# A windowed attention feeding a rational MLP on one core: every engine's order written by hand, the first loads in the order of need, and a prologue of its own

## The chip, the cores and the metric

The kernel runs on one core of one Trainium2 chip. The metric is the device time of one execution in microseconds (us). The kernel before has a median of 319.73 us over three runs (317.39 to 325.65). A program on one core has no second die to compare with, so "fast" means only that a run lies within 1.5% of the fastest of its kernel. The profiled execution of before has a span of 318.6 us; the measured time of an execution lies about 1 to 2 us above its span.

## The reference

```python
B, H, S, D = 4, 8, 768, 64; n_sink, window = 4, 128
keep = (key < n_sink) | ((query - key >= 0) & (query - key < window))
x = softmax(where(keep, q @ k.T / sqrt(D), -1e9)) @ v      # (B*S, H*D) = (3072, 512)
h = x @ w_in                                               # 512 -> 2048
P = a0 + a1*h + a2*h**2 + a3*h**3
Q = 1 + |b0|*|h| + |b1|*h**2
out = (P / (Q + 1e-6)) @ w_out                             # 2048 -> 512, float32
```

## The kernel before

The work goes in 12 steps of 256 tokens. A step has 4 pairs of heads for the attention; the MLP halves a step into two units of 1024 hidden features, so there are 24 units. PE makes scores, the weighted sum of v and both projections; ACT (ScalarE) makes the exponentials, copies h out of PSUM and forms 1/Q as exp(-ln Q); DVE (VectorE) makes the masks, the normalization and the polynomials. One iteration of the program's loop takes one unit from each of several steps in flight, and a scheduler may move instructions of an engine against the text.

```python
ps_hp = ...tile_pool(name="ps_h", bufs=2, space=PSUM)   # first projection
ps_sp = ...tile_pool(name="ps_s", bufs=1, space=PSUM)   # scores
ps_mp = ...tile_pool(name="ps_m", bufs=2, space=PSUM)   # all else, ps_out too
...
def load_q(tile_i):             # GpSimd's queue, cast fp32 -> bf16 on the way; k and v too
    nc.gpsimd.dma_start(out=t_, in_=q[...])
def turn_q(tile_i):             # queries turned by DMA, issued from SP
    nc.sync.dma_start_transpose(out=qT_fix[b % 2][...], in_=q_bf.pop(tile_i)...)
def turn_x(s, grp):             # attention output turned by DMA, issued from SP
    for n in range(NTS):
        nc.sync.dma_start_transpose(out=xblk[s][...], in_=x_n[s][...])
def square(i):                  # half of the squares on each engine
    if i % 2 == 0: nc.scalar.activation(out=sq[i], in_=hb[i], func=AF.Square)
    else:          nc.vector.tensor_tensor(out=sq[i], in0=hb[i], in1=hb[i], op=ALU.mult)
...
for i in range(-3, NU + 4):     # s_q, s_a: the steps whose scores, whose sums are made
    scores(s_q, 2 * grp_q); log_den(i - 1); even(i - 1); odd(i - 1)
    project_in(i, 0); attend(s_a, 2 * grp_a); odd_h(i - 1)
    scores(s_q, 2 * grp_q + 1); recip_den(i - 1); project_in(i, 1)
    attend(s_a, 2 * grp_a + 1); turn_x(s_a, grp_a)
    load_v(s_q + 1); numerator(i - 1); mask(s_q, grp_q)          # conditions cut
    magnitude(i); square(i); denominator(i); project_out(.., 0)
    turn_q(2 * s_q + 3); turn_q(2 * s_q + 4); turn_k(s_q + 1)    # every second iteration
    gate(i - 1); project_out(.., 1)
```

The softmax here doesn't subtract the row's maximum and nothing guards it: scores larger than these inputs give would overflow.

Of the kernel before, what the change touches and what calls it, by code (L numbers as in the profile page):

```python
# [17 lines left out]
def kernel(  # L18
# [13 lines left out]
    nc = tc.nc  # L32
    nc.scalar.preload_act_table_set("natural_log_exp_and_others")
# [17 lines left out]
    NU = 2 * NSTEP  # L51
    inv_sqrt_d = 1.0 / float(D) ** 0.5
# [12 lines left out]
    ps_mp = ctx.enter_context(tc.tile_pool(name="ps_m", bufs=2, space=bass.MemoryType.PSUM))  # L65
# [4 lines left out]
    for n in range(3):  # L70
        t_ = const_pool.tile([P, NPB, NHF, 2, D + 1], BF16, name=f"v_bd_{n}")
        nc.gpsimd.memset(t_, 0.0)
        for e in range(2):
            nc.gpsimd.memset(t_[e * 64:(e + 1) * 64, :, :, e, D:D + 1], 1.0)
        v_fix.append(t_)

    def load_q(tile_i):
        b, T = divmod(tile_i, S // P)
        t_ = a_kv.tile([P, H, D], BF16, tag="q_bf", name="q_bf", bufs=3)
        nc.gpsimd.dma_start(out=t_, in_=q[b, :, T * P:(T + 1) * P, :].rearrange("h p d -> p h d"))  # L80
        q_bf[tile_i] = t_

    def load_k(s):
        b, g = divmod(s, GPB)
        t_ = a_kv.tile([P, NTS, H * D], BF16, tag="k_bf", name="k_bf")
        for t in range(NTS):
            r0 = g * TS + t * P
            nc.gpsimd.dma_start(out=t_[:, t, :].rearrange("p (h d) -> p h d", h=H),  # L88
                                in_=k[b, :, r0:r0 + P, :].rearrange("h p d -> p h d"))
        k_bf[s] = t_  # L90

    def load_v(s):
        b, g = divmod(s, GPB)
        t_ = v_fix[s % 3]
        for h in range(H):
            i, e = divmod(h, 2)
            nc.gpsimd.dma_start(  # L97
                out=t_[e * 64:(e + 1) * 64, i, :, e, 0:D],
                in_=v[b, h, g * TS:(g + 1) * TS, :].rearrange("(j p) d -> p j d", p=64))
        v_bd[s] = t_  # L100
# [3 lines left out]
    nc.sync.dma_start(out=b_bc, in_=moe_b.partition_broadcast(P))  # L104
    a_bc = const_pool.tile([P, 4], FP32, name="a_bc")
    nc.sync.dma_start(out=a_bc, in_=moe_a.partition_broadcast(P))

    for n in range(3):
        load_q(n)
    load_k(0)  # L110
    load_v(0)

# [13 lines left out]

    edge0 = const_pool.tile([P, 2 * NHF, 2, 64], BF16, name="edge0")
    nc.vector.tensor_copy(out=edge0, in_=edge.unsqueeze(1).to_broadcast([P, 2 * NHF, 2, 64]))
    for e in range(2):
        for n in range(2):  # L130
            nc.vector.memset(edge0[e * 64:e * 64 + NS, n * NHF, 0, :], 1.0)
# [11 lines left out]
    sink_edge = const_pool.tile([P, NS], BF16, name="sink_edge")  # L143
    with nc.allow_low_precision(reason="sum of one 1 and zeros"):
        nc.vector.tensor_reduce(out=sink_edge, in_=tri.rearrange("p h c -> p c h"),
                                axis=mybir.AxisListType.X, op=ALU.add)

    babs = const_pool.tile([P, 2], FP32, name="babs")
    nc.scalar.activation(out=babs, in_=b_bc, func=AF.Abs)
    bpos = const_pool.tile([P, 2], FP32, name="bpos")  # L150
    nc.vector.tensor_scalar(out=bpos, in0=babs, scalar1=1e-9, scalar2=None, op0=ALU.max)
    binv = const_pool.tile([P, 2], FP32, name="binv")
    nc.vector.reciprocal(out=binv, in_=bpos)

    csc = const_pool.tile([P, 1], FP32, name="csc")
    nc.vector.tensor_tensor(out=csc, in0=bpos[:, 1:2], in1=binv[:, 0:1], op=ALU.mult)
    cinv = const_pool.tile([P, 1], FP32, name="cinv")
    nc.vector.tensor_tensor(out=cinv, in0=bpos[:, 0:1], in1=binv[:, 1:2], op=ALU.mult)
    qsc = const_pool.tile([P, 1], FP32, name="qsc")
    nc.vector.tensor_tensor(out=qsc, in0=bpos[:, 0:1], in1=cinv, op=ALU.mult)  # L160
    acoef = const_pool.tile([P, 4], FP32, name="acoef")
    nc.vector.tensor_copy(out=acoef[:, 0:1], in_=a_bc[:, 0:1])
    cpow = const_pool.tile([P, 3], FP32, name="cpow")
    nc.vector.tensor_copy(out=cpow[:, 0:1], in_=cinv)
    nc.vector.tensor_tensor(out=cpow[:, 1:2], in0=cinv, in1=cinv, op=ALU.mult)
    nc.vector.tensor_tensor(out=cpow[:, 2:3], in0=cpow[:, 1:2], in1=cinv, op=ALU.mult)
    nc.vector.tensor_tensor(out=acoef[:, 1:4], in0=a_bc[:, 1:4], in1=cpow, op=ALU.mult)
    one_eps = const_pool.tile([P, 1], FP32, name="one_eps")
    nc.vector.memset(one_eps, 1.000001)
    a0, a1, a2, a3 = (acoef[:, n:n + 1] for n in range(4))  # L170


    e_fix = {}
    for grp in range(2):
        for n in range(2):
            t_ = const_pool.tile([P, 2 * NHF * EW + 64], BF16, name=f"e_{grp}_{n}")
            nc.vector.memset(t_, 0.0)
            e_fix[grp, n] = t_
    kT_fix = []
    for n in range(2):  # L180
        t_ = const_pool.tile([P, NPB * NHF, P], BF16, name=f"kT_{n}")
        nc.vector.memset(t_, 0.0)
        kT_fix.append(t_)
    k_sink = []
    for n in range(2):
        t_ = const_pool.tile([P, NPB, P], BF16, name=f"k_sink_{n}")
        nc.vector.memset(t_, 0.0)
        k_sink.append(t_)
    qT_fix = []
    for n in range(2):  # L190
        t_ = const_pool.tile([P, NPB, S + P], BF16, name=f"qT_{n}")
        nc.vector.memset(t_[:, :, S:S + P], 0.0)
        qT_fix.append(t_)

    w_in_sb = [wpool.tile([P, DF], BF16, name=f"w_in_sb_{c}") for c in range(NDMC)]
    w_out_sb = [wpool.tile([P, DM], BF16, name=f"w_out_sb_{c}") for c in range(NFFC)]
    v_sink = const_pool.tile([P, B, H, D + 1], BF16, name="v_sink")
    nc.vector.memset(v_sink, 0.0)

    def load_w_in(half):  # L200
        f0, f1 = half * DF // 2, (half + 1) * DF // 2
        for c in range(NDMC):
            t_f = a_kv.tile([P, DF // 2], FP32, tag="w_in_f", name="w_in_f", bufs=2)
            nc.sync.dma_start(out=t_f, in_=moe_w_in[c * P:(c + 1) * P, f0:f1])
            nc.vector.tensor_scalar(out=w_in_sb[c][:, f0:f1], in0=t_f, scalar1=csc,
                                    scalar2=None, op0=ALU.mult)

    def load_w_out():
        for c in range(NFFC):
            nc.gpsimd.dma_start(out=w_out_sb[c], in_=moe_w_out[c * P:(c + 1) * P, :])  # L210

    def load_v_sink():
        for h in range(H):
            nc.gpsimd.dma_start(out=v_sink[16 * h:16 * h + NS, :, h, 0:D],
                                in_=v[:, h, 0:NS, :].rearrange("b s d -> s b d"))
        for b in range(B):
            nc.vector.tensor_copy(out=v_sink[:, b, :, D], in_=ind)


    def turn_q(tile_i):  # L220
        b, T = divmod(tile_i, S // P)
        nc.sync.dma_start_transpose(out=qT_fix[b % 2][:, :, T * P:(T + 1) * P],
                                    in_=q_bf.pop(tile_i).rearrange("p h d -> p (h d)"))

    def turn_k(s):
# [13 lines left out]
        if g == 0:  # L239
            for i in range(NPB):  # L240
                nc.vector.tensor_copy(
                    out=k_sink[b % 2][:, i, 32 * i:32 * i + 32].rearrange(
                        "p (e s) -> p e s", e=2)[:, :, 0:NS],
                    in_=kT[:, i * NHF, :].rearrange("p (e s) -> p e s", e=2)[:, :, 0:NS])
# [3 lines left out]
    def sink_scores(s):  # L248
# [3 lines left out]
        for i in range(NPB):  # L252
            nc.tensor.matmul(ps[:, c0:TS], lhsT=k_sink[b % 2][:, i, :],
                             rhs=qT_fix[b % 2][:, i, g * TS + c0:(g + 1) * TS],
                             start=(i == 0), stop=(i == NPB - 1))
        t_ = a_x.tile([P, TS], BF16, tag="e_sink", name="e_sink")
# [6 lines left out]
    def scores(s, i):  # L263
# [4 lines left out]
        for n in range(NHF):  # L268
# [3 lines left out]
                             rhs=qT_fix[b % 2][:, i, c:c + 192], start=True, stop=True)  # L272
        data = e_t[:, 64:].rearrange("p (j c) -> p j c", c=EW)[:, il * NHF:(il + 1) * NHF, 0:192]
# [14 lines left out]
    def attend(s, i):  # L288
# [4 lines left out]
        for n in range(NTS):  # L293
# [10 lines left out]
            for m, (l_, r_) in enumerate(terms):  # L304
                nc.tensor.matmul(ps_o[:, n, :], lhsT=l_, rhs=r_.rearrange("p e c -> p (e c)"),  # L305
                                 start=(m == 0), stop=(m == len(terms) - 1))
        if i == 0:
# [12 lines left out]
    def turn_x(s, grp):  # L320
        if grp == 0:
            xblk[s] = xpool.tile([P, NDMC, TS], BF16, tag="xblk", name="xblk")
        for n in range(NTS):
# [6 lines left out]

    def project_in(i, half):
        m, u = divmod(i, 2)
        if half == 0:
            hb[i] = m_sb.tile([P, UW], BF16, tag="hb", name="hb")
        ps_h = ps_hp.tile([P, UC // 2, TS], FP32, tag="ps_h", name="ps_h")
        for n in range(UC // 2):
            fc = u * UC + half * (UC // 2) + n
            for c in range(NDMC):
                nc.tensor.matmul(ps_h[:, n, :], lhsT=w_in_sb[c][:, fc * P:(fc + 1) * P],  # L339
                                 rhs=xblk[m][:, c, :], start=(c == 0), stop=(c == NDMC - 1))  # L340
        w = UW // 2
        nc.scalar.activation(out=hb[i][:, half * w:(half + 1) * w],  # L342
                             in_=ps_h.rearrange("p n c -> p (n c)"), func=AF.Copy)

    def square(i):
        sq[i] = m_sb.tile([P, UW], BF16, tag="sq", name="sq")
        if i % 2 == 0:
# [167 lines left out]
```

## Time and profile before

| | before |
|---|---|
| median time, span | 319.73, 318.6 us |
| first logarithm, fourth logarithm (units 0 and 3) | 61.12, 104.91 us |
| a unit: 3 to 12, 12 to 20 | 10.45, 9.93 us |
| from the last logarithm to the end | 13.0 us |
| DVE, PE, ACT busy | 250.4, 240.5, 212.8 us |

The logarithm of a unit (written lnq) occurs once per unit, so its starts cut the run into fill, units and tail. Most views of before stand in the prediction. In them PE is TensorE, PEld its weight loads, SPq the DMA issues of SyncE. A slice is a fortieth of the span and its digit the busy share in tenths; PEclk is the granted TensorE clock, also in tenths. Three more lines matter later. First, the group of the score matmuls: 192 of them are busy 27.4 us, and PE was idle only 9.4 us just ahead of them, most of that for turned keys (kT).

```profile
L270 PE MATMUL ps_s<-qT,kT 128*128 128x192 bf16 x192 | 27.4, 272 | 9.4 <-DVE kT L237 7.3 <-ACT e L274 1.8
```

Second, SP's issues in order of time (start, duration, queue, line, what): the two last pairs of query turns.

```profile
126.70 2.51 SPq L222 DMA_TRANSPOSE qT<-q_bf  x2
147.85 2.71 SPq L222 DMA_TRANSPOSE qT<-q_bf  x2
```

After 150.6 us before turns no more queries: the scheduler has drawn these issues far ahead of their place in the loop.

### The profile page before, as it was taken

What the parts mean: (1) busy time and instruction counts of PE and PEld (TensorE: products, weight loads), DVE (VectorE), ACT (ScalarE), POOL (GpSimd) and SP (SyncE); (2) the same over time, 40 slices, a digit from 0 to 9 for tenths busy, and PEclk for the clock granted to TensorE, in tenths of its full rate; (3) what the DMA queues carried; (4) which work ended last, traced back from release to release, by engine and by line L of the source; (5) the groups of instructions that cost most, each with busy time, mean ns of one, the idle gap of its engine ahead of it and who ended that gap; (6) DMA issues with size and microseconds to landing.
All of it is one profiled execution on the core that took longest, in us unless ns stands there. A gap on an engine that the chain in (4) does not pass through costs nothing.

```text
span 318.6 us, 5033 instructions
## 1 busy us (share of the span) xinstructions
PE 240.5 (75%) x1920; PEld 167.4 (53%) x1920; DVE 250.4 (79%) x384; ACT 212.8 (67%) x194; POOL 127.1 (40%) x192
## 2 busy tenths in 40 slices
PE   0025448749348969998879989989899898979964
PEld 0014336638224746666647665577575675746521
DVE  7534520769936897899998999999999899897990
ACT  1013014657823993996878978889799897877951
POOL 9986667996884341534540113356200000000000
PEclk9999556979858998999999999999999999999999
DMA  4999999999999996996960627549510111110011
GB/s 132 111 209 192 204 184 151 99 131 103 111 107 136 102 123 84 86 82 86 107 76 17 76 54 56 72 58 107 72 44 22 36 51 49 35 33 33 35 66 66
DMA packets 110775, 28.67 MB, mean 90 GB/s; under 512 B 104608, under 2 KB 106656, under 8 KB 110752
## 3 DMA queue, kind: packets, MB, share of 16 engines
q0 software_dynamic: 78976, 11.56, 58.1%
q1 hardware_dynamic: 31776, 16.79, 23.6%
q8 instruction: 15, 0.25, 0.3%
q14 instruction: 8, 0.07, 0.1%
HBM read 27.30 MB, written 6.29 MB: 105 GB/s over the span
## 4 chain that ended last, share of the span: by engine, by line
DVE 33%; ACT 21%; DMA 19%; PE 10%; issue 7%; POOL 5%; SPq 3%; DVEq 0%; ACTq 0%; POOLq 0%
DMA xblk<-x_n 12%; ACT lnq L379 7%; ACT den L383 6%; DVE den L358 5%; DVE g L388 5%; PE ps_h L339 5%; DVE num L373 4%; DVE sq L370 4%; PE ps_out L398 3%; ACT e L274 3%; SPq L324 3%; DVE den L354 3%; ACT hb L342 3%; DVE num L362 2%; DMA q_bf<-in_q_dram 2%
## 5 line engine op out<-in xcount | busy, mean ns | idle before, releaser
L339 PE MATMUL ps_h<-xblk,w_in_sb 128*128 128x256 bf16 x768 | 98.0, 278 | 30.7 <-DMA xblk<-x_n 30.6
L339 PEld LDWEIGHTS <-w_in_sb 128*128 128x128 bf16 x768 | 74.4, 100 | 45.6 <-DMA xblk<-x_n 28.1
L398 PE MATMUL ps_out<-w_out_sb,g 128*128 128x512 bf16 x384 | 93.5, 391 | 3.7 <-DVE g L388 3.4
L97 POOL DMA_DIRECT2D v_bd<-in_v_dram x96 | 61.8, 663 | 55.4 <-PE ps_o L305 47.3
L274 ACT ACTIVATE e<-ps_s 128x768 bf16<-128x768 f32 x48 | 38.7, 806 | 53.2 <-PE ps_s L270 53.2
L342 ACT ACTIVATE hb<-ps_h 128x1024 bf16<-128x1024 f32 x48 | 48.7, 1018 | 21.1 <-PE ps_h L339 21.1
L398 PEld LDWEIGHTS <-g 128*128 128x128 bf16 x384 | 37.3, 101 | 44.0 <-issue 5.1
L379 ACT ACTIVATE lnq<-den,one_eps,qsc 128x2048 f32<-128x2048 bf16 x24 | 50.2, 2092 | 5.5 <-DVE den L358 5.5
L383 ACT ACTIVATE den<-lnq 128x2048 bf16<-128x2048 f32 x24 | 45.8, 1908 | 0.0
L270 PE MATMUL ps_s<-qT,kT 128*128 128x192 bf16 x192 | 27.4, 272 | 9.4 <-DVE kT L237 7.3
L305 PE MATMUL ps_o<-v_bd,e 128*128 128x130 bf16 x352 | 31.4, 226 | 3.0 <-DMA v_bd<-in_v_dram 1.8
L388 DVE TENSOR_TENSOR g<-num,den 128x2048 bf16<-128x2048 bf16 x24 | 29.4, 1223 | 5.4 <-ACT den L383 5.3
L358 DVE TENSOR_TENSOR den<-den,sq 128x2048 bf16<-128x2048 bf16 x24 | 29.4, 1223 | 2.5 <-ACT sq L348 2.0
L281 DVE TENSOR_TENSOR e<-e,edge 128x1024 bf16<-128x1024 bf16 x24 | 16.2, 675 | 17.7 <-ACT e L274 17.7
L373 DVE TENSOR_TENSOR num<-num,sq 128x2048 bf16<-128x2048 bf16 x24 | 29.3, 1222 | 0.4
L370 DVE TENSOR_TENSOR sq<-sq,hb 128x2048 bf16<-128x2048 bf16 x24 | 29.1, 1214 | 0.1
L305 PEld LDWEIGHTS <-e 128*128 128x128 bf16 x352 | 26.1, 101 | 5.2 <-issue 3.5
L88 POOL DMA_DIRECT2D k_bf<-in_k_dram x24 | 22.2, 931 | 15.9 <-PE ps_kT L232 14.9
L80 POOL DMA_DIRECT2D q_bf<-in_q_dram x24 | 21.7, 906 | 17.2 <-DMA qT<-q_bf 17.2
L270 PEld LDWEIGHTS <-kT 128*128 128x128 bf16 x192 | 18.0, 108 | 16.4 <-DVE kT L237 9.8
L348 ACT ACTIVATE sq<-hb 128x2048 bf16<-128x2048 bf16 x12 | 22.9, 1911 | 0.3
L232 PE MATMUL ps_kT<-ident,k_bf 128*128 128x128 bf16 x96 | 8.1, 233 | 19.9 <-POOL ident masks.py:199 18.9
(56 smaller groups left out, 224.1 us busy)
## 6 DMA issues: line engine op xcount, KB each, us to landing
out_dram<-o_t SPq DMA_DIRECT2D x24, 256.0 KB, 2.1
w_in_f<-in_moe_w_in_dram SPq DMA_DIRECT2D x8, 512.0 KB, 5.8
q_bf<-in_q_dram POOLq DMA_DIRECT2D x24, 128.0 KB, 4.8
k_bf<-in_k_dram POOLq DMA_DIRECT2D x24, 128.0 KB, 4.8
v_bd<-in_v_dram POOLq DMA_DIRECT2D x96, 32.0 KB, 3.8
w_out_sb<-in_moe_w_out_dram POOLq DMA_DIRECT2D x16, 128.0 KB, 6.7
xblk<-x_n SPq DMA_TRANSPOSE x48, 2.5
qT<-q_bf SPq DMA_TRANSPOSE x24, 4.0
```

Of the source, the lines that this page charges most:

```text
L97: nc.gpsimd.dma_start(out=t_[e * 64:(e + 1) * 64, i, :, e, 0:D], in_=v[b, h, g * TS:(g + 1) * TS, :].rearrange("(j p) d -> p j d", p=64))
L270: nc.tensor.matmul(ps[:, n // 2, (n % 2) * 192:(n % 2) * 192 + 192], lhsT=kT_fix[s % 2][:, i * NHF + n, :], rhs=qT_fix[b % 2][:, i, c:c + ...
L274: nc.scalar.activation(out=data.rearrange("p (a n) c -> p a n c", a=2), in_=ps[:, :, 0:384].rearrange("p a (n c) -> p a n c", n=2), func=A ...
L305: nc.tensor.matmul(ps_o[:, n, :], lhsT=l_, rhs=r_.rearrange("p e c -> p (e c)"), start=(m == 0), stop=(m == len(terms) - 1))
L339: nc.tensor.matmul(ps_h[:, n, :], lhsT=w_in_sb[c][:, fc * P:(fc + 1) * P], rhs=xblk[m][:, c, :], start=(c == 0), stop=(c == NDMC - 1))
L342: nc.scalar.activation(out=hb[i][:, half * w:(half + 1) * w], in_=ps_h.rearrange("p n c -> p (n c)"), func=AF.Copy)
L358: nc.vector.tensor_tensor(out=den[i], in0=den[i], in1=sq[i], op=ALU.add)
L373: nc.vector.tensor_tensor(out=num[i], in0=num[i], in1=sq[i], op=ALU.add)
L379: nc.scalar.activation(out=lnq[i], in_=den[i], func=AF.Ln, scale=qsc, bias=one_eps)
L383: nc.scalar.activation(out=den[i], in_=lnq[i], func=AF.Exp, scale=-1.0)
L388: nc.vector.tensor_tensor(out=g_of[m, u], in0=num[i], in1=den[i], op=ALU.mult)
L398: nc.tensor.matmul(ps_out[m, tt], lhsT=g_of[m, u][:, co:co + P], rhs=w_out_sb[fc], start=(fc == 0), stop=(fc == NFFC - 1))
```

## The change

Its intent: give each engine a fixed order, bring the first data in the order in which it is needed, write steps 0 to 2 by hand, and let each part of the elementwise chain start one unit after its projection, so that no engine waits for work of the same iteration.

```diff
+    ctx.enter_context(tc.manual_schedule())
-    ps_mp = ...(name="ps_m", bufs=2, space=PSUM)
+    ps_mp = ...(name="ps_m", bufs=1, space=PSUM)
+    ps_op = ...(name="ps_o", bufs=1, space=PSUM)        # ps_out alone
 def load_q / load_k / load_v:
-        nc.gpsimd.dma_start(...)                        # cast on the way
+        nc.sync.dma_start(fp32 tile) for steps 0..2, cast later on ACT (q) or DVE (k, v)
 def scale_w_in(half):
-            nc.vector.tensor_scalar(out=w_in_sb[c]..., in0=t_f, scalar1=csc, ...)
+            nc.gpsimd.tensor_scalar(out=w_in_sb[c]..., in0=w_f[half, c], scalar1=csc, ...)
 def turn_q: q tiles 0..6 on PE (transpose, copy by DVE); turn_x: steps 0 and 1 on PE
 def square(i):
-        if i % 2 == 0:                                  # ACT, else DVE
+        if i % 4 != 3:
... (constants moved, GpSimd's and DVE's start reordered)
+def iteration(i):
+    store(..)                                           # ACT copy of ps_out, one iteration late
+    scores(s_q, 2 * grp_q); exps(..)
+    chain_1(i - 1)                                      # magnitude, square if i%4==3, denominator
+    project_in(i, 0); log_den(i - 1); copy_in(i, 0)
+    attend(s_a, 2 * grp_a); gate(i - 2); normalize(..)
+    project_in(i, 1); scores(s_q, 2 * grp_q + 1); exps(..)
+    even(i - 1); odd(i - 1); recip_den(i - 1)
+    attend(s_a, 2 * grp_a + 1); normalize(..); turn_x(s_a, grp_a)
+    copy_in(i, 1); project_out(.., 0); odd_h(i - 1); mask(s_q, grp_q)
+    if grp_q == 0: sink_scores(s_q); sink_exps(s_q); load_v(s_q + 1); feed(s_q + 2)
+    if grp_q == 1: turn_qs(s_q + 1); turn_k(s_q + 1)
+    numerator(i - 1); square(i); project_out(.., 1)
+# prologue: casts, turns, scores, attends of steps 0..2 written out (110 lines)
```

## The prediction

> **What bounds the kernel now.** I read the slices first, then the same thing in windows, then the queues, the waits, and the row of one ScalarE instruction in order of time.
>
> ```profile
> PE   0025448749348969998879989989899898979964
> DVE  7534520769936897899998999999999899897990
> PEclk9999556979858998999999999999999999999999
> DMA  4999999999999996996960627549510111110011
> ```
>
> One slice is 8 us. Up to slice 13 (104 us) PE is broken up and its clock is often 5 to 8 tenths; the DMA engines are full. After slice 15 PE and DVE are both at 8 to 9. So there are two kernels: a fill bound by waits for data, and a balanced steady part. Two windows of the steady part (length, then busy time and count of each engine; PEclk, DMA share, GB/s last):
>
> ```profile
> 120.00:200.00 80.00, 73.12 (x618) 51.41 (x616) 73.31 (x107) 64.71 (x60) 26.80 (x39) 0.99 0.72 75
> 200.00:290.00 90.00, 82.56 (x700) 58.71 (x698) 85.83 (x124) 75.94 (x70) 13.92 (x21) 1.00 0.32 51
> ```
>
> DVE is 95% busy in the second, ACT 84%. The work comes in 24 units (half a step each) with one logarithm (lnq) per unit; its starts are the kernel's pulse:
>
> ```profile
> 61.12 2.09 ACT L379 ACTIVATE lnq<-den,one_eps,qsc 128x2048 f32<-128x2048 bf16 x1
> ...
> 104.91 2.09 ACT L379 ACTIVATE lnq<-den,one_eps,qsc 128x2048 f32<-128x2048 bf16 x1
> ...
> 198.92 2.08 ACT L379 ACTIVATE lnq<-den,one_eps,qsc 128x2048 f32<-128x2048 bf16 x1
> ...
> 278.34 2.10 ACT L379 ACTIVATE lnq<-den,one_eps,qsc 128x2048 f32<-128x2048 bf16 x1 [0.81 <-DVE den L358]
> ...
> 305.56 2.10 ACT L379 ACTIVATE lnq<-den,one_eps,qsc 128x2048 f32<-128x2048 bf16 x1 [0.99 <-DVE den L358]
> ```
>
> These are units 0, 3, 12, 20 and 23. The span of 318.6 is 61.1 of fill, 3 units at 14.6, 9 at 10.4, 8 at 9.93, 3 at 9.07 (attention has ended), and 13.0 of tail. Had all ran at 9.93 after unit 0, 18 us would be saved; the fill holds more.
>
> The waits of the fill (total, times, longest) and the queues (packets, MB, share of 16 engines over the span):
>
> ```profile
> PE ps_h L339 <- DMA xblk<-x_n: 30.6, 14, 8.9
> PE ps_kT L232 <- POOL ident masks.py:199: 18.9, 1, 18.9
> PEld L232 <- DMA k_bf<-in_k_dram: 15.6, 1, 15.6
> ```
> ```profile
> q0 software_dynamic: 78976, 11.56, 58.1%
> q1 hardware_dynamic: 31776, 16.79, 23.6%
> ```
>
> The first transpose waits 15.6 us for keys and then to 18.9 us for an identity that GpSimd makes after 13 load issues and six memsets of v_bd. The projection waits 30.6 us for turned x, 21.4 of it before 120 us: with both queues full the x transpose took up to 7.4 us to land, against a median of 2.5. All q, k and v loads go through q0: 58.1% of 318.6 us x 16 / 78976 is 37.5 ns a packet, so one step of 6144 packets costs that queue 14.4 us, and it is busy until about 165 us.
>
> **What the Trainium skill says.** "DMA: Bandwidth & Descriptors", SWDGE vs HWDGE vs iDMA: only the software path (GpSimd) casts in flight, and the two paths feed different internal queues of one engine, served in turn. The trace agrees: the casting loads are all in q0, and where q0 and q1 both run (60 to 75 us) the DMA share is 1.93. So fp32 loads on the hardware queue add a lane but need a cast afterwards. "TensorE: Matmul & The Clock Gate", Part 4: a PE transpose ends in PSUM and needs a copy by DVE; here ps_kT does (684 ns a copy of 1024 columns). Same page, Part 1: PE idling brings the half clock back; the clock above dips so. "GPSIMD Engine Reference", 4.1: one-input work is roughly line-rate there, so I take 1 to 2 us for a 128x1024 scale, an estimate; no row of before has one.
>
> **The change part by part.** It takes the order of every engine from the text (before, a scheduler chose it; the instruction lists of the two differ in nearly every line, though in number hardly: PE 3930 rows against 3842, DVE 355 in both). It loads q, k and v of steps 0 to 2 as fp32 through the hardware queue in the order of need and casts them on ACT and DVE; turns q tiles 0 to 6 and x of steps 0 and 1 on PE instead of by DMA; moves the w_in scaling to GpSimd, half of DVE's squares to ACT, and ps_out to a bank of its own (so the other small PSUM tiles share one bank in place of two); and starts the polynomial of a unit one iteration after its projection. I work out three stretches. "Hops" are the 0.1 to 0.2 us from one engine's end to the next one's start, as between kT's copy at 22.07 and the scores at 22.13, taken generously.
>
> *Fill.* (a) The first issue of keys moves from 9.9 to about 1.3 us, of queries from 6.8 to about 2.2. The same five transfers took 10.4 us in before (6.82 to 17.2); 1.3 + 10.4, plus 2 for v sharing the engines, gives 14. (b) Cast on ACT 0.6, four transposes 0.5, copy about 0.4 (half of ps_kT's 0.684 and a fixed part), hops 0.5: 16. The identity is first on GpSimd now, so that wait is gone. (c) Four score rounds on the single ps_s: the exps of step 0 start 1.7 us apart in before, so 6.9: 23. (d) Four attends through a now single ps_m bank: about 1.0 cold matmuls, 0.18 + 0.42 on DVE, 0.3 hops, 1.9 each, 7.6; two PE turns of x at 1.2: 33. That replaces transposes by DMA that ended at 44.3 and 49.6. (e) Projection 32 matmuls at 0.17 cold (38 took 6.34): 5.5; copy 1.0, square 1.9, den 1.2, hops: 43. w_in needs 2 MB at about 200 GB/s after the queries, near 24, and four scales, near 30: hidden. I allow 3 us for the second step's keys: first lnq at 46 against 61.1. **Saving 15.**
>
> *Units 0 to 3.* Between lnq 0 and 1 DVE does 4 normalizations 2.4, two copies 0.9, two masks 1.4, the polynomial 4.1, casts and kT 3.2, queries 0.9, den 1.9: 14.8. Then 10.5 and 10 with loads still dense: 35 against 43.8. **Saving 9.**
>
> *Steady part.* Removed from DVE: half of its 12 squares, 0.25 x 1.22 = 0.30 a unit; 9.06 units in 90 us gave 85.83 / 9.06 = 9.47, now 9.2. Added to ACT: 0.25 x 1.91 = 0.48 on 8.38, now 8.9. PE by spacing, since its ends are modelled:
>
> ```profile
> 293.37 3.66 PE L339 MATMUL ps_h<-xblk,w_in_sb 128*128 128x256 bf16 x32
> 296.86 7.07 PE L398 MATMUL ps_out<-w_out_sb,g 128*128 128x512 bf16 x32
> ```
>
> Taking off the last one's length, 0.109 and 0.216 us apart: 32 and 16 per unit give 3.5 + 3.45; 18 ps_o at 0.068 are 1.2, 8 ps_s 0.64, kT and sink 0.4: 9.2. Three engines at 9.2, 9.2, 8.9, each waiting for the others in a fixed order: I choose 5% over the largest, 9.65. Nine units at 9.65 instead of 10.45 and eight instead of 9.93: **saving 7 and 2.** Three late units at 8.7: **1.** The tail (ln 2.1, exp 1.9, gate 1.2, 16 matmuls 3.6, copy 0.6, store) keeps its chain: 13.
>
> Sum: 46 + 35 + 86.9 + 77.2 + 26.1 + 13 = 284; the time lies 1.1 above the span (319.73 and 318.6): **285 us**.
>
> Beside the path: DVE loses 6.0 of w_in scaling and gains about 11.5 of casts and copies, all in the fill where it idled.
>
> **Rivals.** *A load-bound fill.* The hardware queue now carries 19456 packets of q, k, v and the w_in in order, with six shared stage buffers: a late cast blocks all behind it, and w_out waits for the keys of step 2. At 37.5 ns a packet steps 0 to 2 take 45 us and w_in about 10, so step 2 lands near 57 and step 3, behind w_out, near 80. For it: DMA is at 9 today. Against: two queues overlap. It would cost 8 to 12 us: 295. *Head-of-line stalls in the fixed order.* One ps_m bank and one ps_out bank make PE wait for DVE and ACT inside each unit; then units stay at 9.93 or reach 10.3: 290 to 297. Against: scores, projections and attends alternate so that a copy has other matmuls beside it. *ACT as the bound.* Three units in four carry a square: 8.38 - 0.96 + 1.91 is 9.3 there, under 9.65. *All better:* 9.3 a unit and lnq 0 at 42: 274.
>
> **Range and chances.** The fill may miss by 8, the unit by 0.35 x 17 = 6; not both the same way as a rule: 273 to 300. Slower than 313 needs the fill gain lost and a worse unit: faster 0.93, same 0.04, slower 0.03.
>
> **What would show it.** lnq 0 near 46 and lnq 3 near 81; then 9.65 apart; the PE waits for xblk down from 30.6 to under 10; PEclk full from about 45 us; ACT about 229 busy. I am wrong if lnq 0 comes after 55 with PE waiting for k, q or v loads, or if units stay above 10 with PE waiting for ps_m or ps_out.

## The result and the profile after

The changed kernel takes 350.19 us in the median of four runs (347.17 to 356.97, the last of them slow), against 319.52 for before in the same rounds. A ratio here is the mean time of one kernel's fast runs over that of the other's fast runs of the same rounds, so it is not quite the ratio of the medians; it is 1.095 (95% interval 1.086 to 1.104). The change is slower by 9.5%. The profiled span is 345.5 us.

The slices (8.6 us each here), then one steady window, in the same columns as the prediction shows for before:

```profile
PE   0446575274886797958874997796869979979675
PEclk9999859558699699969998799999998999999989
```

```profile
200.00:290.00 90.00, 76.03 (x648) 54.83 (x646) 76.78 (x109) 74.55 (x68) 22.41 (x31) 0.98 0.48 65
```

PE starts earlier than in before, but then no engine is full: in 90 us of the steady part DVE works 76.78 us against 85.83 before. Something between the engines makes all of them wait. The logarithms say where:

```profile
50.43 2.09 ACT L457 ACTIVATE lnq<-den,one_eps,qsc 128x2048 f32<-128x2048 bf16 x1 [2.51 <-DVE den L436]
...
102.94 2.10 ACT L457 ACTIVATE lnq<-den,one_eps,qsc 128x2048 f32<-128x2048 bf16 x1 [2.56 <-DVE den L436]
...
214.16 2.08 ACT L457 ACTIVATE lnq<-den,one_eps,qsc 128x2048 f32<-128x2048 bf16 x1
...
303.27 2.09 ACT L457 ACTIVATE lnq<-den,one_eps,qsc 128x2048 f32<-128x2048 bf16 x1 [0.81 <-DVE den L436]
```

These are units 0, 3, 12 and 20. Set against before:

| stretch | before | predicted | after | after less predicted |
|---|---|---|---|---|
| to lnq 0 | 61.1 | 46 | 50.4 | +4.4 |
| units 0 to 3 | 43.8 | 35 | 52.5 | +17.5 |
| units 3 to 12 | 94.0 | 86.9 | 111.2 | +24.3 |
| units 12 to 20 | 79.4 | 77.2 | 89.1 | +11.9 |
| units 20 to 23 | 27.2 | 26.1 | 26.8 | +0.7 |
| tail | 13.0 | 13 | 15.4 | +2.4 |

So 10.7 us were won by the first logarithm, and all but 2.0 of them lost again by the fourth; a unit then takes 12.36 and 11.14 us instead of 10.45 and 9.93. The group of the score matmuls names the place:

```profile
L319 PE MATMUL ps_s<-qT,kT 128*128 128x192 bf16 x192 | 28.7, 276 | 36.7 <-DMA qT<-q_bf 15.0 <-ACT o_t L482 6.9 <-ACT e L331 6.3
```

PE idles 36.7 us ahead of scores instead of 9.4: 27.3 us more, nearly the whole loss of 30. The releaser named first is the turned queries (qT), for 15.0 us. The rest is put down to other engines, and the list alone doesn't show that it has the same cause; the first experiment does. The list of waits has two lines that were not among the long ones of before:

```profile
DVE rec L374 <- PE ps_o L362: 42.0, 34, 5.3
PE ps_s L319 <- DMA qT<-q_bf: 15.0, 8, 4.5
```

DVE now waits 42.0 us for attention sums (8.4 before): work that stands behind the late scores in the fixed order. The chain of waits (start, duration, what) shows how one step's hold-up comes about:

```profile
229.84 0.43 DVE x_n L376
...
230.32 1.17 SPq L397
...
231.54 1.24 SPq L397
...
232.87 1.22 SPq L266
...
234.18 2.41 DMA qT<-q_bf
...
236.64 0.33 PE ps_s L319 x2
```

DVE finishes a normalized x. SP issues two DMA turns of x (L397), 1.2 us each, and only then the turns of the next step's queries (L266), which had been ready (in this run SP never waits for loaded queries there). The first scores of the next iteration stand at the head of PE's order and need those queries. PE therefore waits for a chain that begins with its own last attend. In before the last pair of query turns was issued from 147.85 us on; here the last turn starts at 278.95:

```profile
255.83 2.53 SPq L266 DMA_TRANSPOSE qT<-q_bf  x2
278.95 1.22 SPq L266 DMA_TRANSPOSE qT<-q_bf  x1
```

### The profile page after: what moved, and what is told of

Same layout as the page of the kernel before. It is cut to its first block, busy times and chain, and to the rows that moved or that the text cites. A ratio compares the mean times of both kernels' runs of the same rounds, so it can differ in the third digit from the quotient of the medians.

```text
span 345.5 us, 5116 instructions
## 1 busy us (share of the span) xinstructions
PE 254.3 (74%) x1964; PEld 178.7 (52%) x1964; DVE 254.7 (74%) x372; ACT 229.1 (66%) x207; POOL 127.6 (37%) x165
## 3 DMA queue, kind: packets, MB, share of 16 engines
HBM read 27.30 MB, written 6.29 MB: 97 GB/s over the span
## 4 chain that ended last, share of the span: by engine, by line
PE 38%; DVE 19%; ACT 18%; DMA 13%; SPq 5%; issue 4%; ACTq 0%; DVEq 0%
PE ps_h L412 21%; PE ps_o L362 7%; DMA xblk<-x_n 5%; DMA qT<-q_bf 5%; ACT lnq L457 4%; ACT den L461 4%; PE ps_s L319 4%; PE ps_out L477 4%; ACT hb L420 4%; SPq L397 4%; DVE den L436 3%; ACT sq L426 3%; DVE sq L448 3%; DVE x_n L376 2%; ACT e L331 2%
## 5 line engine op out<-in xcount | busy, mean ns | idle before, releaser
L412 PE MATMUL ps_h<-xblk,w_in_sb 128*128 128x256 bf16 x768 | 106.3, 297 | 11.6 <-DMA xblk<-x_n 11.5
L412 PEld LDWEIGHTS <-w_in_sb 128*128 128x128 bf16 x768 | 79.8, 106 | 28.8 <-DMA xblk<-x_n 14.0
L477 PE MATMUL ps_out<-w_out_sb,g 128*128 128x512 bf16 x384 | 91.0, 384 | 4.9 <-ACT o_t L482 4.9
L127 POOL DMA_DIRECT2D v_bd<-in_v_dram x72 | 47.3, 673 | 101.8 <-PE ps_o L362 99.3
L477 PEld LDWEIGHTS <-g 128*128 128x128 bf16 x384 | 36.7, 99 | 43.0 <-issue 7.7
L319 PE MATMUL ps_s<-qT,kT 128*128 128x192 bf16 x192 | 28.7, 276 | 36.7 <-DMA qT<-q_bf 15.0
L374 DVE RECIPROCAL rec<-ps_o 128x4 f32<-128x4 f32 x48 | 8.7, 181 | 42.0 <-PE ps_o L362 42.0
L362 PE MATMUL ps_o<-v_bd,e 128*128 128x130 bf16 x352 | 32.8, 233 | 5.8 <-DVE x_n L376 4.0
L426 ACT ACTIVATE sq<-hb 128x2048 bf16<-128x2048 bf16 x18 | 34.4, 1913 | 0.4
L245 POOL TENSOR_SCALAR w_in_sb<-w_in_f,csc 128x1024 bf16<-128x1024 f32 x8 | 24.3, 3046 | 2.1 <-DMA w_in_f<-in_moe_w_in_dram 1.9
L376 DVE TENSOR_TENSOR x_n<-ps_o,rec 128x256 bf16<-128x256 f32 x48 | 20.4, 425 | 1.7
```

Of the source, the lines that this page charges most:

```text
L127: nc.gpsimd.dma_start(out=t_[lo:hi, i, :, e, 0:D], in_=src)
L319: nc.tensor.matmul(ps[:, n // 2, (n % 2) * 192:(n % 2) * 192 + 192], lhsT=kT_fix[s % 2][:, i * NHF + n, :], rhs=qT_fix[b % 2][:, i, c:c + ...
L362: nc.tensor.matmul(ps_o[:, n, :], lhsT=l_, rhs=r_.rearrange("p e c -> p (e c)"), start=(m == 0), stop=(m == len(terms) - 1))
L412: nc.tensor.matmul(ps[:, n, :], lhsT=w_in_sb[c][:, fc * P:(fc + 1) * P], rhs=xblk[m][:, c, :], start=(c == 0), stop=(c == NDMC - 1))
L477: nc.tensor.matmul(ps_out[m, tt], lhsT=g_of[m, u][:, co:co + P], rhs=w_out_sb[fc], start=(fc == 0), stop=(fc == NFFC - 1))
```

## The experiments

All fourteen kernels gave correct results. The median of a kernel is over all its runs; those of the change, after_sched and g_fill2_banks hold one slow run each, those of before up to three. Not all groups ran on the same chip, so a difference between two groups is only as good as before's agreement in them (319.5 to 320.8). Before was measured beside each group of runs on the same chip: 320.75, 319.9, 319.92, 320.32 and 320.08 us in the five groups. Times are medians. One kernel that I wanted could not be run: before with the scheduler turned off and nothing else changed. Its text order deadlocks when simulated, so what the bare order of before would cost is open.

| kernel | built on | us | ratio to before |
|---|---|---|---|
| q_early | change | 330.65 | 1.037 (1.028 to 1.045) |
| x_early | change | 356.97 | 1.113 (1.101 to 1.124) |
| q_x_early | change | 355.76 | 1.116 |
| after_sched | change | 337.24 | 1.053 (1.044 to 1.062) |
| q_gate | q_early | 314.34 | 0.985 (0.979 to 0.990) |
| q_pe_x | q_early | 329.88 | 1.033 (1.026 to 1.039) |
| q_banks | q_early | 325.49 | 1.020 (1.013 to 1.026) |
| q_fill | q_early | 331.27 | 1.037 |
| g_fill2 | q_gate | 303.92 | 0.954 (0.946 to 0.963) |
| g_sq | q_gate | 317.28 | 0.996 (0.988 to 1.003) |
| g_banks | q_gate | 305.13 | 0.958 (0.949 to 0.966) |
| g_fill2_banks | g_fill2 | 301.09 | 0.943 (0.936 to 0.950) |
| g_gate_first | g_fill2_banks | 309.28 | 0.970 (0.963 to 0.978) |
| g_sq_split | g_fill2_banks | 297.84 | 0.931 (0.923 to 0.940) |

**q_early: the query turns go ahead of the x turns.**

```diff
 def iteration(i):
+    if has_q and grp_q == 1 and s_q + 1 < NSTEP:
+        turn_qs(s_q + 1)
     ...
     if has_q and grp_q == 1 and s_q + 1 < NSTEP:
-        turn_qs(s_q + 1)
         turn_k(s_q + 1)
```

> The changed kernel with the two DMA turns of q issued at the start of the iteration instead of behind the turn of x; nothing else moved. Theory 1 (the slowdown is the q turn standing last in the SP order: x_n, two x turns of 2.46 us, then a q turn of 1.2 and 2.4 to land, and PE cannot pass the scores that wait for it): a step of 23.0 us loses some 3 us, nine steps, so about 322 us (318 to 328), PE's idle before the scores from 36.7 to about 10. Theory 2 (one bank each for the small PSUM tiles and for ps_out, in a fixed order): no more than 5 us gained, 345 or more. Theory 3 (loads that crowd the DMA engines): the wait moves to x or to loads, 340 or more.

330.65 us: 19.5 less than the change, by moving two issues (18.1 between the means of the fast runs). The time misses the 318 to 328 expected, but the wait goes where it was expected to go. PE's idle time ahead of the scores falls from 36.7 us to

```profile
L319 PE MATMUL ps_s<-qT,kT 128*128 128x192 bf16 x192 | 27.1, 270 | 9.6 <-ACT e L331 6.3 <-DVE kT L281 3.3
```

so the waits that the profile had put down to other engines went with the query turns. That their place behind the x turns is a main cause is thus shown. The wait for turned x rises from 11.5 to 21.2 us, as the third theory had it. What is left is uneven: many units take 9.9 us, but some 12 to 15. At each of those PE waits for turned x:

```profile
208.29 3.09 PE L412 MATMUL ps_h<-xblk,w_in_sb 128*128 128x256 bf16 x14 [4.47 <-DMA xblk<-x_n]
```

The turn it waited for took 6.29 us to land, while a window from 205 to 209 us has a mean DMA share of 2.29, the highest of the neighbourhood. GpSimd had issued v, keys and queries of later steps from 199.3 to 204.7 us, released by the same attends that release the turn of x.

**x_early: attends, normalization and turn of x ahead of the second half of the projection.**

```diff
+    attend(s_a, 2 * grp_a)              # ahead of project_in(i, 0)
     project_in(i, 0) ...
+    attend(s_a, 2 * grp_a + 1)          # ahead of project_in(i, 1)
+    even(i - 1)
+    normalize(s_a, 2 * grp_a + 1); turn_x(s_a, grp_a)
     project_in(i, 1) ...
```

> The changed kernel with both attends of an iteration, their normalizations and the turn of x placed before the second half of the projection and its scores; the turn of q still behind that of x. Theory 1 extended (the loop is x_n, then DMA turns, then the next iteration's first PE work, for x in one iteration and for q in the other): both chains begin about 2 us earlier in every iteration, so about 2 us times some 18 iterations at most, 315 to 330 us. Theory 2 (shared PSUM banks): the two attends now follow each other on one bank with the gate between, so it gets slower, 352 or more.

356.97 us, slower than the change (by 6.6 us between the means of the fast runs; the intervals of the two ratios overlap a little). The two attends now follow each other, and both use the one ps_m bank:

```profile
PE ps_o L362 <- DVE x_n L376: 35.2, 19, 3.6
```

In the change this wait was 4.0 us. The stall at the small bank that the prediction had as a rival is thus real, but only in an order without other matmuls between two attends. The change's own order avoids it.

**q_x_early: both together.** The edit is the sum of the two.

> Both moves together. Theory 1: what is left is the balanced work, some 9.6 us a unit, with the slow fill (lnq 3 at 103 us) and the tail of the changed kernel: 103 + 17 x 9.65 + 3 x 8.9 + 15 is 309 (302 to 318). Theory 2: no faster than the better of the two alone.

355.76 us, the same as x_early: the bank wait (41.6 us in this run) seems to hide what the early queries gain. PE's idle time ahead of the scores does fall, from 18.4 us in x_early to 8.8.

**after_sched: the change without the line that switches the scheduler off.**

```diff
-    ctx.enter_context(tc.manual_schedule())
```

> The changed kernel with the one line taken out that keeps the order as written, so that the scheduler orders every engine as it did for the kernel before; loads, casts, PE turns, banks and the split of squares stay as changed. If the order is at fault: about 310 (300 to 322), below before, since the early loads then pay. If the single PSUM banks or the loads are at fault: 335 or more.

337.24 us, where about 310 was expected if the order alone was at fault. The steady part comes back to nearly that of before: 10.17 us a unit from 12 to 20 (9.93 before, 11.14 in the change). But the fill is worse than that of either kernel: lnq 0 at 64.25 and lnq 3 at 118.25. The written order is therefore not the only thing that costs; the other parts of the change, under the old scheduler, cost 13 us by the fourth unit. One of them is visible there: PE waits 14.7 us in this run for w_in scaled on GpSimd. In the change the same row is

```profile
L245 POOL TENSOR_SCALAR w_in_sb<-w_in_f,csc 128x1024 bf16<-128x1024 f32 x8 | 24.3, 3046 | 2.1 <-DMA w_in_f<-in_moe_w_in_dram 1.9 <-POOL v_bd L188 0.2
```

3.05 us each, against 765 ns on DVE before.

**q_gate: the loads wait until x is turned.** GpSimd copies two elements of the turned x to a spare tile before it issues the loads, so the loads start behind the turn instead of beside it.

```diff
             if s_q + 1 < NSTEP:
+                hold = a_x.tile([P, 2], BF16, tag="hold", name="hold")
+                nc.gpsimd.tensor_copy(out=hold, in_=xblk[s_a][:, 3, P - 1:P + 1])
                 load_v(s_q + 1)
```

> As q_early (330.65 us there), plus one GpSimd copy that reads the turned x of a step before GpSimd issues the next v, k and q loads, so that those loads no longer start together with the x turn that PE waits for. Theory A (in q_early PE waits 21.2 us for x in 10 places because the loads are released by the same attends and crowd the turn): the waits fall to about 5 us and the time to 316 to 322. Theory B (the turn is late in itself: SP issue 2.46 and 2.4 to land): the waits stay near 20 us, 328 or more; if held loads come too late, PE waits for k or v instead and it gets slower.

314.34 us, 16.3 less than q_early and less than before. Between 100 and 300 us the wait for turned x falls from 19.7 us (nine waits, longest 4.5) to

```profile
PE ps_h L412 <- DMA xblk<-x_n: 7.4, 9, 1.3
```

and a unit from 3 to 20 from 10.89 to 10.03 us. The number of waits is the same; each is shorter. That the collision of loads and turns was the second cause is thereby shown. I had not thought of it before the experiments.

**q_pe_x: x of all steps turned on PE, no DMA turn of x.**

```diff
-    NS_PE = 2
+    NS_PE = 12
```

> As q_early, with x of all steps turned on PE through the small PSUM bank and a DVE copy, none by DMA. Theory A and B both take the 21.2 us of x waits away, and what is added is 20 copies of 0.425 us on DVE (8.5 us) and 80 transposes on PE: 314 to 322. Theory 2 (the single small bank binds): the added use of that bank costs as much as it saves, 328 or more.

329.88 us, no gain over q_early, on which it is built. The wait for the DMA is gone and another has its place:

```profile
PE ps_xT L392 <- DVE x_n L376: 26.5, 24, 1.5
```

PE must turn x right behind DVE's normalization and has nothing else at the head of its order: 24 waits of about 1.1 us. The time is the one that the theory of the single small bank expected (328 or more). But x_n is the data of the turn and its writing also frees the bank, so this wait doesn't tell the two apart.

**q_banks: two rotating banks shared by the small tiles and ps_out, as before.**

```diff
-    ps_mp = ...(name="ps_m", bufs=1, ...); ps_op = ...(name="ps_o", bufs=1, ...)
+    ps_mp = ...(name="ps_m", bufs=2, ...)
```

> As q_early, with the two small banks put back as one rotating pair shared by attends, turns, sink scores and ps_out, as in the kernel before. If the single bank for attends and turns binds (theory 2), 322 or less; if not, within 3 us of 330.65, or slower because ps_out now holds one of the pair through two calls.

325.49 us, 5.2 less than q_early, between the two expectations. The gain is in the fill (lnq 0 at 46.56 for 49.93, lnq 3 at 92.26 for 99.33) and in the tail (13.9 us for 17.0). The uneven units remain and take half of it back: 11.19 us a unit from 3 to 20, for 10.89.

**q_fill: the polynomial of unit 0 moved behind the keys, scores and masks of step 2 in the prologue.**

```diff
     copy_in(1, 1)
-    even(0); odd(0); odd_h(0); numerator(0)
     square(1)
     ...
     cast_v(2)
+    even(0); odd(0); odd_h(0); numerator(0)
```

> As q_early, with the polynomial of unit 0 (4 DVE instructions, 4.1 us) moved behind the cast and turn of the third step's keys, its queries, scores and mask. Theory (the fill is a serial chain: PE idles from 59 to 64 us because the cast of k stands behind the polynomial on DVE, and lnq 1 comes 27 us after lnq 0): lnq 1 comes 3 to 4 us earlier and the time is 326 to 328. Rival (PE or loads bind there): no change.

331.27 us, no gain: lnq 1 comes at 78.43 instead of 76.94. Moving one block back leaves the chain as long as it was.

**g_fill2: the prologue of q_gate rewritten.** The casts and turns of the next step stand between the attends of this one, and the turns use the bank of ps_out, which is free in the fill.

```diff
+    attend(0, 0); normalize(0, 0); cast_k(1); turn_k(1, spare=True)
+    attend(0, 1); normalize(0, 1); cast_q(3); turn_q(3, spare=True); turn_x(0, 0)
+    attend(0, 2); normalize(0, 2); cast_q(4); turn_q(4, spare=True)
+    attend(0, 3); normalize(0, 3); turn_x(0, 1)
... (scores of step 1, then the polynomial of unit 0 in pieces between
     the attends of step 1, with the casts and turns of step 2)
```

> On top of q_gate (314.34 us, span 311.7): only the hand-written prologue is rewritten. Casts and turns of the next step's keys and queries stand between the attends of the step before, the turns of the prologue use the bank of ps_out as a second one, the polynomial of unit 0 is cut into pieces between the attends. Theory (the fill is a serial chain through one bank and one order, not a load wait): the stretch from the first logarithm to the second falls from 26.2 us to about 15 to 18, the first stays near 50, and the time to about 303 (297 to 307). Rival (the fill is bound by loads and by the scaling of w_in on GpSimd, which ends near 44 us): the first two logarithms move by less than 3 us and the time stays at 312 to 316.

303.92 us, 10.4 less. The time is as expected, the parts only roughly: from lnq 0 to lnq 1 it is still 19.5 us (15 to 18 expected), and lnq 0, expected to stay near 50, is earlier too. lnq 0 comes at 46.22, lnq 1 at 65.68 (77.25 in q_gate), lnq 3 at 87.88 (99.01). The wait in the change's fill was a chain, one link of which reads like this in PE's rows (last column: idle time and its releaser):

```profile
64.20 1.03 PE L276 MATMUL ps_kT<-ident,k_bf 128*128 128x128 bf16 x8 [5.21 <-DVE k_bf L113]
66.81 0.58 PE L263 MATMUL ps_qT<-ident,q_bf 128*128 128x128 bf16 x4 [1.57 <-DVE kT L281]
67.91 0.59 PE L263 MATMUL ps_qT<-ident,q_bf 128*128 128x128 bf16 x4 [0.52 <-DVE qT L264]
```

Each turn waits for DVE to empty the single ps_m bank, and the first for a cast that stands late on DVE. From 60 to 120 us PE worked at a granted clock of 0.74 in the change; in g_fill2 it is 0.94. It was not a wait for keys: the three casts of keys waited 0.9 us in all for their loads.

**g_sq: the squares shared half and half again, on q_gate.**

```diff
-        if i % 4 != 3:        # ACT
+        if i % 2 == 0:
```

> On top of q_gate: the squares shared half and half by ACT and DVE as in the kernel before (3 of 4 on ACT in the change). If DVE is the bound of the steady units, as the prediction took it, this gives back 0.25 x 1.22 = 0.3 us a unit: +5 to +7 us, about 320. If units are set by chains between engines and not by DVE's work, within 2 us of q_gate, 312 to 317. If ACT were the bound: 305 to 310.

317.28 us, 2.9 more: just outside what I had called "no change", and short of the 5 to 7 us that DVE as the bound would cost. A unit from 2 to 20 is 10.15 us against 10.11 in q_gate; most of the rest lies in fill and tail. Moving a quarter of the squares from ACT to DVE hardly moves the unit, so neither engine's work, summed over all units, sets it. What sets a single unit is taken up in the last run.

**g_banks: two rotating banks, on q_gate.**

> On top of q_gate: the small PSUM tiles and ps_out share two rotating banks, as in the kernel before. On top of q_early this was worth 5 us, all in the fill. Theory (one bank costs only in the fill and the tail): about 309 (306 to 312), with the first logarithm near 46.5, and units 2 to 20 at the 10.1 us of q_gate. Rival (the banks also cost in the steady part and were hidden there by late x turns): units fall to 9.8 or less and the time to 303 to 305.

305.13 us, 9.2 less, more than expected: lnq 0 at 46.72, lnq 3 at 92.81 (99.01), tail 13.8 for 15.3. Units 2 to 20 take 10.13 us, as expected: in the steady part the bank is worth nothing.

**g_fill2_banks: both mends of the fill.** The edit is the sum of the two.

> g_fill2 (303.92 us, span 302.7) with two rotating banks for the small PSUM tiles and ps_out. If the order of the prologue and the bank removed the same wait of the fill, the first logarithms stay at 46, 66 and 76 and the gain is the tail alone: in g_fill2 the last unit waits 3.6 us for the one ps_out bank and then runs at a low clock, 17.8 us from the last logarithm's start to the end against 13.8 in g_banks, so -4: about 300 (298 to 302). If they are two different waits: the third logarithm before 72 and about 294 to 296. If the tail's low clock in g_fill2 was chance: 303.

301.09 us in the median of six runs (five fast, from 299.95 to 304.26), 2.8 less than g_fill2. The tail is 13.9 us against 17.8. In g_fill2 the last unit ran into the one ps_out bank:

```profile
289.44 9.66 PE L477 MATMUL ps_out<-w_out_sb,g 128*128 128x512 bf16 x32 [3.63 <-ACT o_t L482]
```

The gains of the two mends overlap: alone they are 10.4 and 9.2, together 13.3. The profiled run is 3 us above the median of its kernel and has lnq 1 at 69.52, so I do not read its fill closely. The two kernels that follow have the same prologue and banks, with lnq 1 at 66.54 and 65.47 and lnq 2 at 77.06 and 75.64. That is the first alternative: order and bank removed largely the same wait.

**g_gate_first: DVE's product g (1.22 us) moved ahead of the next denominator.**

```diff
+    gate(i - 2)
     chain_1(i - 1)
     ...
     attend(s_a, 2 * grp_a)
-    gate(i - 2)
```

> g_fill2_banks with one line moved: DVE's multiplication g (1.22 us a unit) stands ahead of the magnitude and the denominator of the next unit instead of behind them, so that it runs while DVE waits for ACT's square (1.15 us of idle in every second unit of g_fill2). Same work on all engines. Ring theory (square on ACT, denominator on DVE, logarithm on ACT, in a fixed order): units fall from 10.1 to about 9.5 to 9.8, and the time by 5 to 10 us against g_fill2_banks. Rival (DVE's or ACT's work with the fixed costs of an instruction is already full at 10.1): units stay within 0.1 of 10.1 and the time within 2 us. Third way: the denominator now comes later on DVE in the units where DVE is late, and units rise to 10.4 or more.

309.28 us, 8.2 more: the third way. A unit from 2 to 20 takes 10.45 us. DVE's idle time before the denominator only shrinks from 1.15 to 0.96 us, and where DVE is late anyway the logarithm now waits longer. The theory that g would fit into a gap fell. The trace of g_fill2_banks suggested a new one: units alternate. In the interval that ends with lnq 14 DVE has no idle time (10.12 us; the key turn's copies are in it). In the one that ends with lnq 13 ACT has none (9.78 us), and DVE idles 1.15 us for ACT's square.

**g_sq_split: the square of every odd unit cut in two, half on ACT, half on DVE.**

```diff
 def square(i):
-    if i % 4 != 3: ACT, whole; else DVE, whole
+    w = UW if i % 2 == 0 else UW // 2
+    nc.scalar.activation(out=sq[i][:, 0:w], in_=hb[i][:, 0:w], func=AF.Square)
 def chain_1(i):
     magnitude(i)
-    if i % 4 == 3: square(i)
+    if i % 2 == 1: sq[i][:, w:UW] = hb[i][:, w:UW] ** 2 on DVE
     denominator(i)
```

> g_fill2_banks with the square of every odd unit cut in two, half on ACT and half on DVE, where ACT did it whole in units 1, 5, 9 ... and DVE whole in units 3, 7, 11 ...; the total of each engine's work stays (a little more, for the fixed part of two instructions instead of one). If alternating full engines set the unit (DVE full in the units with a key turn, 10.1; ACT or DVE full in the others, 9.8), the intervals into the odd units fall from 9.8 to about 9.35 and the others stay: about 4 us less than g_fill2_banks, 296 to 298. If a fixed chain of hand-overs or the sum of DVE's work sets it: no change, within 1.5 us of g_fill2_banks (300 to 302.5), or a little more.

297.84 us, within the 296 to 298 expected, 3.3 less than g_fill2_banks and 6.9% less than before. The logarithms of units 12 to 14, in g_fill2_banks and then in g_sq_split:

```profile
181.50 2.10 ACT L456 ACTIVATE lnq<-den,one_eps,qsc 128x2048 f32<-128x2048 bf16 x1 [0.43 <-DVE den L435]
191.28 2.10 ACT L456 ACTIVATE lnq<-den,one_eps,qsc 128x2048 f32<-128x2048 bf16 x1
201.40 2.10 ACT L456 ACTIVATE lnq<-den,one_eps,qsc 128x2048 f32<-128x2048 bf16 x1 [0.57 <-DVE den L435]
```

```profile
176.67 2.10 ACT L459 ACTIVATE lnq<-den,one_eps,qsc 128x2048 f32<-128x2048 bf16 x1 [0.55 <-DVE den L438]
186.01 2.10 ACT L459 ACTIVATE lnq<-den,one_eps,qsc 128x2048 f32<-128x2048 bf16 x1 [0.51 <-DVE den L438]
196.23 2.10 ACT L459 ACTIVATE lnq<-den,one_eps,qsc 128x2048 f32<-128x2048 bf16 x1 [0.68 <-DVE den L438]
```

The interval into the odd unit falls from 9.78 to 9.34 us, where 9.35 was expected; the one into the even unit stays (10.12 and 10.22). The work was only evened, not lessened. Of the eight intervals into odd units between units 4 and 20 six fall to 9.3; those into units 9 and 15 take 10.5 (9.88 and 11.01 in g_fill2_banks). In g_sq, with these squares whole on DVE, most odd intervals are 9.86: shifting the square doesn't help, halving it does. So the unit of about 10 us is a mean of two unlike units. That the odd one is set by its fuller engine is what this run shows. For the even one it is argued only: in g_fill2_banks PE is as busy in the interval to lnq 14 as DVE (9.82 and 9.86 of 10.12 us), and no run separates them.

## Why the prediction was wrong

The prediction said 285 us and gave 3% to "slower". The step that failed worst is the steady part; the fill comes next. Point by point:

**"Three engines at 9.2, 9.2, 8.9, each waiting for the others in a fixed order: I choose 5% over the largest, 9.65."** This step failed. The works were about right (in q_gate, without the two hold-ups, 180 to 280 us hold 92.69 us of DVE and 90.66 of ACT; at 10.05 us a unit that is 9.3 and 9.1 a unit). But the unit took 11.78 us from 3 to 20, and 17 units at 2.13 too much are 36 of the 61 us that the prediction missed. In the profiled runs they divide as follows. The query turns issued behind the x turns: 11.78 to 10.89, 15 us (q_early). The loads issued beside the x turns: 10.89 to 10.03, 14.5 us (q_gate). The remainder, 10.03 to 9.65, 6.5 us: I take it that the 5% was too little because a unit with key turns and one without are unlike, and averages hide that. This third part is shown only in part: g_sq_split took 0.44 to 0.53 us off six of the eight odd units, and its mean from 3 to 20 is still 9.90.

**What I had not read.** The prediction treats the DMA turns of x and queries as hidden, and it follows only PE, DVE and ACT through the new order. The issuing engine, SP, is also in a fixed order now. In before the scheduler had moved the last query turns some 100 us ahead of their place; the written loop took that away. The difference of instruction orders and SP's rows of before were at hand and would have shown it.

**The rival "head-of-line stalls in the fixed order ... 290 to 297".** Its name was right and its place wrong. It named PE waiting for the ps_m and ps_out banks. The change's steady units wait for turned queries. Bank waits turned up in x_early, in the fill and in the tail. **The test "units stay above 10 with PE waiting for ps_m or ps_out"** came true in its first half only.

**"lnq 0 at 46", saving 15.** Measured 50.43, saving 10.7. The terms (a) to (e) kept to the plan or ran ahead of it: the projection, predicted at 33, starts at 31.41. The term that was short is the last, "I allow 3 us for the second step's keys":

```profile
31.41 5.03 PE L412 MATMUL ps_h<-xblk,w_in_sb 128*128 128x256 bf16 x32
37.54 1.91 ACT L426 ACTIVATE sq<-hb 128x2048 bf16<-128x2048 bf16 x1
48.45 0.69 DVE L432 TENSOR_SCALAR den<-hb 128x1024 uint32<-128x1024 uint32 x1
```

The square ends at 39.45, and DVE takes the magnitude (den) only 9.0 us later. In the written order it stands behind the second step's keys, queries, scores, mask and cast of v, a chain in which DVE itself works 2.97 us of the 9.0. Where that work is moved between the attends and the projection (g_fill2), den follows the square by 0.3 us and lnq 0 stands at 46.22. With two banks it stands at 46.72 (g_banks). So the 4.4 us come from the order of the prologue and the bank.

**"Between lnq 0 and 1 DVE does ... 14.8", "35 against 43.8".** This step failed. The interval between lnq 0 and 1 was 26.9 us, the next two 12.2 and 13.4, all three 52.5. DVE's work was right (14.63 us of those 26.85), but it was taken for the length of the stretch. The stretch is a chain: cast, turn on PE, copy, next turn, scores, with one bank. The rewritten prologue took 11.6 us off lnq 1 (g_fill2 against q_gate). That edit also gave the turns a second bank, so its two halves are not separated fully; two banks alone took 6.8 off (g_banks), and the overlap of the two says that they are largely the same wait. The best kernel has lnq 3 at 86.95, still 6 us behind the predicted 81; I did not look for these 6.

**"I take 1 to 2 us for a 128x1024 scale."** The scale took 3.05 us. In the change it was hidden as the prediction said (the first four end at 29.9 us, the projection starts at 31.4), though with 1.5 us to spare. In q_banks, where x is turned sooner, PE waits 0.9 us for it, and under the scheduler 14.7.

**The tail, "keeps its chain: 13".** It took 15.4 us: the store of one half had to empty the one ps_out bank before the next matmuls. With two banks it is 13.8.

**The load-bound fill (295), ACT as the bound.** Neither came. The keys of step 2, put "near 57" by that rival, had landed by 43.75 us, when GpSimd reads them to release the loads of w_out. ACT is busy 229.1 us, where "about 229" was predicted. "PE waits for xblk from 30.6 to under 10" was nearly right (11.5), and "PEclk full from about 45 us" wrong: a mean of 0.74 from 60 to 120 us. The count "DVE 355 in both" can't be checked here: the traces hold 384 and 372 DVE instructions. Nothing rests on it.

What stays open: what the order of before would cost without a scheduler, which of PE and DVE sets the even unit, the last 6 us of the fill, and how much of after_sched's slow fill is the scaling on GpSimd.

## What to carry to other kernels

Before you write an engine's order by hand, list what the scheduler had moved far from its place in the text, above all the issues of DMAs on the engine that issues them, and put those ahead by hand: two lines in the wrong place cost 18 to 19.5 us here. Look for transfers on the critical path and bulk loads that are released by the same event. Here they collided, and letting the loads wait for the transfer gained 16 us without less traffic. When several engines are nearly full, work out the largest engine of each kind of unit instead of the largest average, and even the work between kinds of units before you move it between engines.

## What the Trainium skill lacked or had wrong

- "GPSIMD Engine Reference", 4.1 Engine selection, calls one-input elementwise work there roughly line-rate. A scale of 128x1024 fp32 to bf16 by a per-partition scalar took 3046 ns on GpSimd and 765 ns on DVE: four times as long.
- "DMA: Bandwidth & Descriptors", Rules for kernel authors, says: "A transpose next to ordinary DMAs needs nothing". The sentence stands in a rule about correct results, and in that sense it held in all runs. What the page lacks is the time: in q_early a turn of x landed in a median of 2.4 us, and in 6.29 us beside loads of v, keys and queries. Making the loads wait gained 16.3 us.
- No page that I read gives in time what SP spends on issuing a DMA transpose from SBUF to SBUF on this chip; the DMA page has only cycle counts of "previous generations", in its part on trn3. In the changed kernel's chain it was 1.17 to 1.24 us each, one after the other. So two turns of x delay the query turn behind them by 2.4 us before any data moves.
